# A gate that keeps its logits in PSUM, and the order of work where attention meets the first MoE layer

## The chip, the core and the metric

The kernel runs on one core of one Trainium2 chip. The metric is the device time of one execution in microseconds (us), the median of three. The engines are called by the profile's names: PE multiplies matrices (its weight loads, PEld, overlap it), DVE and POOL do elementwise work, ACT does activations and copies, SP issues DMAs. POOL also issues the indirect DMAs that scatter rows. Each engine has one queue of its own and works through it in order; it waits on semaphores that other engines raise.

## The reference

Three layers follow each other. The first is attention masked by clusters: queries and keys are assigned to the nearest of 16 centroids of their head, and a score counts only where both have the same one.

```python
mask = q_assign[:, :, :, None] == k_assign[:, :, None, :]
scores = np.where(mask, scale * np.matmul(q, k.transpose(0, 1, 3, 2)), -1e9)
attn = np.exp(scores - np.max(scores, axis=-1, keepdims=True))
attn /= np.sum(attn, axis=-1, keepdims=True) + 1e-09
x = np.matmul(attn, v)                 # 2 x 8 heads x 768 tokens x 64
```

The second is a mixture of 8 experts (MoE) over the 1536 tokens with 512 columns. A noisy gate picks two experts for each token:

```python
noisy = x @ w_gate + np.log1p(np.exp(x @ w_noise)) * noise
top2 = np.argpartition(-noisy, 2, axis=1)[:, :2]     # weights: softmax of the two
out[mask] += top2_w[mask, k, None] * (np.maximum(x[mask] @ w1[e], 0) @ w2[e])
```

The third is a soft mixture: 32 slots, each a weighted mean of all tokens, go through 8 experts and are mixed back. The change does not touch it.

## The kernel before, in words

**Attention.** The 16 heads are worked through as 8 pairs `p`, each in 12 steps `t` (two halves `qh` of the queries, six blocks `kc` of the keys). One loop runs over the steps `s0 = 0, 2, ..., 96`, two steps to a turn. A turn emits, in this order: up to three units of masked maxima for a pair to come (`munit`: PE writes `pmx`, L333, and DVE reduces it to `mp`, L338 and L343), the scores of its two steps (`psc`, L372 and L374), the products with V of the two steps before (`av`, L387, into the PSUM tile `pav`), the adds of the exponentials `pt` for the denominators (`add`: `psa` on POOL, `psb` on DVE, L404 and L407), and then what the tables `post` hold for these steps: `ot_evac` (ACT copies `pav` out), `den` (PE sums `psa` and `psb` over partitions into `pden`, L434; DVE takes the reciprocal `rd` from `dt`, L437 to L440), `xout` (PE `px`, L451; DVE writes the tokens' columns `x` and the partial gate logits `gp`, L454 and L457). The last two turns compute no masked maxima.

**Gates.** `gate(q, ...)` returns a list of small operations. Gate 0 covers the six chunks of 128 tokens of the first batch, gates 1 and 2 the three and three of the second. All operations of a gate but four on ACT are DVE operations on SBUF tiles, at line 567. `rank` counts on PE, for each token and expert, the tokens ahead of it (`prank`, L615 to L618). With the ranks, `scatter` (L638) sends rows of `x` to the experts' lists `xg` in DRAM, 128 rows of one chunk and one choice at a time. These operations lie in one list `todo`. `gap(s, n)` takes up to `n` of them out of it, and is called five times in a turn; an integer in the list ends a call, and so spaces the operations.

**First MoE layer.** It has 80 steps in ten jobs of eight; jobs 0 and 1 are the short lists, 256 rows each, of the first experts. A step loads 128 columns' weights (`load_w`), splits them into a high and a low part (`split_hi` on ACT, L833, and `split_lo` on DVE or POOL, L840), multiplies the rows by both (`first`, `ph`, L935), applies the ReLU with high and low parts `H` (L941 and L944), and multiplies back (`second`, `py`, L976). The rows of a job come from `xg` (`load_x`, L856), are transposed on DVE (`prep_t`, L890) and split as well (`prep_h` on ACT, L897; `prep_l`, L903). Before, six steps' weights are split, and the rows of jobs 0 and 1 are loaded and split, in the last pair's turns.

The order of all work is written out by hand in this way; what decides is each engine's own queue.

Of the kernel before, what the change touches and what calls it, by code (L numbers as in the profile page):

```python
# [52 lines left out]
PH, PL = 1, 1  # L53
JT, JN, JH, JL = (0, 2), 2, 2, 3
SP = 1, 3, 5, 7, 8, 9
SL, MX = 1, 96
LT = 6, 8, 9
B1 = 9
B7 = 8
B2 = 1  # L60
TF = (0, 0), (0, 1)
RATE = 2, 1, 1, 1, 2, 3, 1, 2, 1, 1, 4, 1, 3
ORD, U1, Z1, R1, Z0 = (1, 1, 1, 0, 1, 0, 1, 1), 3, 8, 4, 2
M2S = 14, 15, 16, 18, 20
MS = 10, 10, 12, 14, 18
G0, GN, KS = 55, 3, 64

# [17 lines left out]
class Attention:  # L85
# [294 lines left out]
    def av(self, p, t):  # L380
        nc, g = self.nc, self.g
        qh, kc = divmod(t, 6)
        pt = self.ptile[p, t]
        if kc == 0:
            self.avp[p, qh] = g.psum.tile([128, 512], F32, tag="av", name="pav")
        for hh in range(2):
            nc.tensor.matmul(self.avp[p, qh][64 * hh:64 * hh + 64, :384], self.vt[p][:, hh, kc, :],  # L387
                             pt[:, hh, :], start=(kc == 0), stop=(kc == 5))

    def add(self, p, t):  # L390

# [28 lines left out]
    def bank(self, p, qh, name):  # L420
        g = self.g
        if p == NP - 1 and qh == 0:
# [39 lines left out]
class Dispatch:  # L462
# [68 lines left out]
    NFILL = (NSL // 128 + 1) // 2 + (NTOK + NTRASH) // 256  # L531

    def gate(self, q, first, n):

        nc, g, xp = self.nc, self.g, self.g.xp
        b = first // (NCK // B)
# [3 lines left out]
        T = {}  # L540
        place = g.place if q == 0 else g.again

        def t(name, *shape, dt=F32):
            if name not in T and q != 1:
# [3 lines left out]
                names = " ".join("abc"[:len(shape)])  # L548
                a = place(m) if dt is F32 else place(m // 2).bitcast(dt)
                T[name] = a.rearrange(f"p ({names}) -> p {names}", **dict(zip("abc", shape)))  # L550
# [54 lines left out]
        op(TTn, wcol(2), TT, wcol(1), op=OP.mult)  # L605
        out.append(3 if b == 0 else 1)
# [22 lines left out]
        op(TR, Q, W2, axis=AX.X, op=OP.add)  # L629
        if b == 0:  # L630
            op(dv.memset, c1[:, 0:NREG], 0.0)
        op(dv.tensor_copy, self.idx[:, :, cs], Q)
# [143 lines left out]
class MoE1:  # L776
# [567 lines left out]
def body(tc, qk, q2, k2, v2, cent, wgn, noise, w12, phi, v12, out):  # L1344
    nc = tc.nc
    with ExitStack() as ctx:
# [93 lines left out]
        for p in range(-1, NP):  # L1440
# [24 lines left out]
            if p >= 0:  # L1465
                for qh in range(2):
                    at(post, s0 + 6 * qh + 6, A.ot_evac, p, qh)
                    for s, fn in zip(LT if p == NP - 1 else (8, 10, 12), (A.total, A.den, A.xout)):
                        at(post, s0 + 6 * qh + s, fn, p, qh)
# [22 lines left out]
        mix(G0, gates[0][0], [], 1)  # L1492
        for f in gates[0][1]:
            todo += [(G0, None)] * GN + [(G0, f)]
        half = len(todo)

        a, z = gates[1][0], [f for f in gates[2][0] if type(f) is not int]
        i = next(i for i, f in enumerate(a) if type(f) is int and i > 10) - 13
        a, x = a[:i], [f for f in a[i:] if type(f) is not int]
        y, z = z[:21], z[21:]  # L1500
        mix(MX, a, [], 1)
        turns = y[:2] + x[:3] + y[2:6] + x[3:6]
        x, y = x[6:], y[6:]
        while x or y:
            turns += x[:1] + y[:1]
            x, y = x[1:], y[1:]
        mix(99, turns, [], 1)
        k = next(i for i, f in enumerate(z) if f.__name__ == "rank")
        mix(99, z[:k] + [1] + z[k:], gates[1][1], 3)
        mix(99, [], gates[2][1], 1)  # L1510
        half = len(todo) - half
        quota = {1: (8, 16), 2: (14, 14), 3: (14, 14)}

# [22 lines left out]
        def load_x(j):  # L1536
            assert len(todo) <= half, (len(todo), half)
            M1.load_x(j)

        for j in range(2):  # L1540
            at(post, s0 - 4, load_x, j)
            s = s0 + JT[j]
            for i in range(JN):
                at(post, s + i, M1.prep_t, j, i, JN)
                at(post, s + i + JH, M1.prep_h, j, i, JN)
                at(post, s + i + JL, M1.prep_l, j, nc.vector if i % 2 else nc.gpsimd, i, JN)
        end = 12 * NP + 2
        for s0 in range(0, end, 2):
            k = RATE[s0 // 2 - 28] if 56 <= s0 < 82 else 1 if s0 < KS else 3 if s0 < 12 * NP else 0
            units = pre.get(s0, []) + pre.get(s0 + 1, [])  # L1550
# [9 lines left out]
            gap(s0, k)  # L1560
            if s0 == 12 * NP:
                M1.first(0)
            for s in (s0 - 2, s0 - 1):
                if 0 <= s < 12 * NP:
                    A.av(*divmod(s, 12))
                    A.add(*divmod(s, 12))
            for s in (s0, s0 + 1):
                for fn, a in post.get(s, ()):
                    fn(*a)
                gap(s0, k)  # L1570
        late = [x for s in sorted(post) if s >= end for x in post[s]]
        c_at.close()
# [6 lines left out]
        for j in range(2):  # L1579
            at(prep, 5 + j, M1.prep_m, j)  # L1580
        for j in range(2, len(M1.jobs)):
            s, n, eng = PREP[j if j in PREP else 4]
# [7 lines left out]
        for s in range(ns):  # L1590
# [12 lines left out]
            if s < NREG * NF:  # L1603
                gap(1000 if s else 98, quota.get(s, (8, 8))[0])
            if s == ns - 1:
# [3 lines left out]
            elif s < ns - 3 and s != NREG * NF - 1:  # L1609
                M1.second(s)  # L1610
            if s < 2:
                fn, a = late[s]
                fn(*a)
            if s < NREG * NF:
                gap(1000 if s else 98, quota.get(s, (8, 8))[1])
            if s == OV:
# [106 lines left out]
```

## Time and profile before

| what | us |
|---|---|
| median of three executions | 644.04 (643.37 to 644.43) |
| the profiled execution | 650.09 |
| its span, first to last instruction | 648.3 |
| PE busy in the span | 614.9 (95%) |
| DVE, ACT and POOL busy in the span | 409.0, 311.3 and 289.3 |

The rows come from the one profiled execution, and the times from others. The mean granted clock of PE in it was 0.981 of full speed. With PE busy for 95% of the span, its idle time is what an engine beside it can cost.

### The profile page before, as it was taken

The page shows a single profiled execution, that of the slowest core. Times are in us where ns is not written, and L with a number is a line of the kernel's source. Part 1 is how long each engine was busy: PE and PEld are TensorE (multiplying, and loading weights), DVE is VectorE, ACT ScalarE, POOL GpSimd, SP SyncE. Part 2 cuts the span into 40 slices and gives each one's busy share as a digit, 9 for nine tenths or more (in the row PEclk, how much of TensorE's full clock was granted, in tenths as well). Part 3 has the DMA queues.
Part 4 walks back from the last instruction along what each step waited for, and adds up shares of the span by engine and source line. Part 5 has one row for each costly group of instructions (what it writes and reads, how often), then busy time and mean ns, then how long its engine had stood idle before and what let it go on. Part 6 is the DMA issues. An engine that isn't in the chain of part 4 may idle for free. (4 is left out here: it accounts for less than half of the span.)

```text
span 648.3 us, 11039 instructions
## 1 busy us (share of the span) xinstructions
PE 614.9 (95%) x3967; PEld 472.8 (73%) x3967; DVE 409.0 (63%) x871; ACT 311.3 (48%) x444; POOL 289.3 (45%) x256
## 2 busy tenths in 40 slices
PE   7899999999799999789999999999999999998996
PEld 5567666676566657667888888888888888875544
DVE  6667888778965798566554445554544557645632
ACT  5576585765556582245334334443534445533002
POOL 3899676866758793543124033251423403110100
PEclk8699999999899999989999999999999999999999
DMA  8392845727255713478944829879796868978995
GB/s 317 76 267 79 287 149 179 252 89 275 95 191 167 209 66 131 156 223 232 196 133 110 218 98 272 298 255 258 278 281 234 167 207 276 321 269 271 425 398 198
DMA packets 62890, 139.47 MB, mean 215 GB/s; under 512 B 15280, under 2 KB 30832, under 8 KB 60784
## 3 DMA queue, kind: packets, MB, share of 16 engines
q1 hardware_dynamic: 56944, 125.31, 58.3%
q0 software_dynamic: 5888, 13.42, 9.5%
q8 instruction: 32, 0.52, 0.3%
q14 instruction: 26, 0.21, 0.1%
HBM read 108.18 MB, written 28.42 MB: 211 GB/s over the span
## 5 line engine op out<-in xcount | busy, mean ns | idle before, releaser
L976 PE MATMUL py<-ring,H 128*128 128x512 f32 (+1 forms) x686 | 172.9, 396 | 5.3 <-issue 3.5
L840 DVE TENSOR_TENSOR ring<-wr,ring 128x1024 fp32r<-128x1024 f32 (+1 forms) x77 | 93.5, 1214 | 100.4 <-ACT ring L833 99.5
L976 PEld LDWEIGHTS py<-ring,H 128*128 128x128 f32 (+1 forms) x686 | 123.9, 184 | 32.5 <-issue 3.8
L833 ACT ACTIVATE ring<-wr 128x1024 fp32r<-128x1024 f32 x77 | 81.5, 1059 | 91.7 <-PE py L976 83.6
L377 ACT ACTIVATE pt<-psc 128x768 f32<-128x768 f32 x96 | 77.2, 811 | 71.1 <-PE psc L374 60.8
L984 POOL DMA_INDIRECT x2acc<-y,mdi x31 | 50.2, 1621 | 104.4 <-ACT y L1009 97.6
L387 PE MATMUL pav<-pt,vt 128*64 128x384 f32 x384 | 73.6, 505 | 0.0
L941 ACT ACTIVATE H<-ph 128x256 fp32r<-128x256 f32 (+7 forms) x80 | 36.7, 459 | 75.9 <-PE ph L935 60.9
L338 DVE TENSOR_REDUCE mp<-pmx 128x1 f32<-128x512 f32 x96 | 63.2, 676 | 15.3 <-PE pmx L333 14.4
L935 PE MATMUL ph<-XS1a,ring 128*128 128x240 f32 (+3 forms) x288 | 67.8, 325 | 0.0
L407 POOL TENSOR_TENSOR psa<-psa,pt 128x768 f32<-128x768 f32 x32 | 61.9, 1936 | 4.7 <-ACT pt L377 2.5
L935 PE MATMUL ph<-XS0a,ring 128*128 128x432 f32 (+3 forms) x252 | 63.2, 332 | 0.1
L944 DVE SCALAR_TENSOR_TENSOR H<-ph,H 128x384 fp32r<-128x384 f32 (+2 forms) x120 | 43.4, 389 | 26.3 <-ACT H L941 20.6
L935 PEld LDWEIGHTS ph<-XS1a,ring 128*128 128x128 f32 x288 | 47.7, 188 | 3.6 <-DVE ring L840 0.2
L935 PE MATMUL ph<-XS0b,ring 128*128 128x256 f32 (+3 forms) x192 | 48.2, 325 | 0.8 <-DVE ring L840 0.6
L935 PE MATMUL ph<-XS1b,ring 128*128 128x240 f32 (+3 forms) x192 | 46.1, 313 | 0.8 <-DVE ring L840 0.8
L935 PEld LDWEIGHTS ph<-XS0a,ring 128*128 128x128 f32 x252 | 43.2, 188 | 4.0 <-issue 1.2
L903 POOL TENSOR_TENSOR XS0b<-xr,XS0a 128x512 fp32r<-128x512 f32 (+1 forms) x9 | 17.1, 1901 | 64.5 <-ACT XS0a L897 64.5
L387 PEld LDWEIGHTS pav<-pt,vt 128*64 128x64 f32 x384 | 23.5, 137 | 24.8 <-issue 19.3
L333 PE MATMUL pmx<-even 96*128 96x512 f32 (+1 forms) x96 | 34.0, 415 | 6.2 <-DVE mp L338 4.3
L343 DVE TENSOR_REDUCE mp<-pmx 128x2 f32<-128x512 f32 x48 | 33.0, 689 | 5.5 <-PE pmx L333 5.0
L638 POOL DMA_INDIRECT xg<-x,idx x24 | 25.9, 1077 | 21.1 <-DVE xr L567 14.8
(338 smaller groups left out, 1023.7 us busy)
## 6 DMA issues: line engine op xcount, KB each, us to landing
wr<-in_w SPq DMA_DIRECT2D x80, 512.0 KB
v<-in_v SPq DMA_DIRECT2D x9, 2048.0 KB
xg<-xr SPq DMA_DIRECT2D x14, 512.0 KB
wr<-in_qk SPq DMA_DIRECT2D x8, 768.0 KB
early<-in_q SPq DMA_DIRECT2D x8, 768.0 KB
early<-in_k SPq DMA_DIRECT2D x8, 768.0 KB
x2acc<-xr SPq DMA_DIRECT2D x8, 512.0 KB
vt<-in_v SPq DMA_DIRECT2D x8, 384.0 KB
```

What stands on the lines that cost most here:

```text
L333: nc.tensor.matmul(o, self.BQ[i][:96, qh, hh, 128 * c:128 * c + 128], self.BK[i][:96, hh, ks], start=True, stop=True)
L338: nc.vector.tensor_reduce(mp[:, 0, col:col + 1], ps, axis=AX.X, op=OP.max)
L377: nc.scalar.activation(pt, ps[:, :, :384], AF.Exp, scale=SCALE)
L387: nc.tensor.matmul(self.avp[p, qh][64 * hh:64 * hh + 64, :384], self.vt[p][:, hh, kc, :], pt[:, hh, :], start=(kc == 0), stop=(kc == 5))
L407: eng.tensor_tensor(s, s, pt.pop((p, t)), op=OP.add)
L833: self.nc.scalar.activation(self.ring[s][0], self.wr[s], AF.Copy)
L840: nc.vector.tensor_tensor(lo[:, :n], wr[:, :n], f32(hi)[:, :n], op=OP.subtract)
L935: nc.tensor.matmul(ph[:, :u], a[:, 128 * c:128 * c + 128], x[:, c, :u], start=(c == 0 and i == 0), stop=(c == 3 and i == 2))
L941: nc.scalar.activation(HH[:, :u], ph[:, :u], AF.Relu)
L944: nc.vector.scalar_tensor_tensor(o[:, :b - a], ph[:, a:b], 0.0, f32(HH)[:, a:b], op0=OP.max, op1=OP.subtract)
L976: nc.tensor.matmul(o, x, y, start=(f == 0 and i == 0), stop=(f == NF - 1 and i == 2))
L984: st = nc.gpsimd.indirect_dma_start(out=out, out_offset=bass.IndirectOffsetOnAxis(ap=di, axis=0), in_=y, in_offset=None, compute_op=OP.add)
```

## The change

Gate 0 becomes a function of its own. Its logits, and the working tile beside them, lie in PSUM: in the columns 384 to 512 of the bank whose columns 0 to 384 hold `pav`. That bank is now allocated once and used by all pairs. Sixteen operations stay on DVE, some twenty go to POOL, and integers space the list.

Of the twelve scatters of gate 0 two stay where the gate ends, and ten are set into the last pair's turns (`SC`, steps 82 to 90). `load_x` of jobs 0 and 1 follows them at step 91 (it was 80). Job 0 is prepared at steps 94 to 96, all `prep_l` on DVE, and job 1 not before the MoE steps 2 to 4. Four steps' weights are split ahead, where it was six.

In the last half of the last pair the last `pt` is not added on DVE: `pden` takes it as a third term. `den` and `xout` of that half come before the first MoE step, where they were behind it. The first operations of gate 1 come at the steps 94 to 97, the rest up to its `rank`, and four more, around the first MoE step. Five filler matmuls ahead of gate 1's `rank` are gone.

```diff
+        if (p, t) == (0, 0):
+            bank = g.psum.tile([128, 512], F32, tag="av", name="pav")
+            self.avb, g.spare = bank[:, :384], bank[:, 384:]
         if kc == 0:
-            self.avp[p, qh] = g.psum.tile([128, 512], F32, tag="av", name="pav")
+            self.avp[p, qh] = self.avb
...
-        if kc == first:
+        if kc == first or (p, t) == (NP - 1, 11):
             return
...
+        if (p, 6 * qh + 5) in self.ptile:
+            parts.append(self.ptile.pop((p, 6 * qh + 5)))
...
+    def gate0(self, n):
...
+        PL, PW = (lambda i=i: g.spare[:, 8 * n * i:8 * n * i + 8 * n].rearrange("p (c e) -> p c e", e=E) for i in range(2))
...
+        op(TR, U, gl(1), axis=AX.X, op=OP.add)
+        op(TR, PL, gl(0), axis=AX.X, op=OP.add)
+        out.append(1)
+        op(act, U, U, lambda: AF.Exp)
+        out.append(1)
+        op(PS, W, U, 1.0, None, op0=OP.add)
+        out.append(3)
...
+        op(PT, N, N, self.noise[:, :n], op=OP.mult)
+        out.append(3)
+        op(TTn, PL, N, PL, op=OP.add)
+        top(M0, PL)
+        op(TTn, PW, PL, lambda: bcn(M0()), op=OP.is_equal)
+        op(TTn, PW, PW, bce(self.iode), op=OP.mult)
+        top(V0, PW)
+        op(TTn, oh[0], PW, lambda: bcn(V0()), op=OP.is_equal)
+        op(STT, PL, oh[0], -1e30, PL, op0=OP.mult, op1=OP.add)
+        op(PS, wcol(0), V0, -1.0, float(E), op0=OP.mult, op1=OP.add)
...
-            for i in range(5 if q == 1 else 0):
-                nc.tensor.matmul(ps[:, 384:], g.ident, g.ident, start=True, stop=True)
...
-        n = 512 if self.short[self.steps[s][0]] and not 6 <= s < 13 and s < DL else 1024
+        n = 512 if self.short[self.steps[s][0]] and 13 <= s < DL else 1024
...
+        for f, s in zip(gates[0][1][2:], SC):
+            at(post, s0 + s, f)
...
-            at(post, s0 - 4, load_x, j)
...
+            at(post, s0 + JX, load_x, j)
+        for i in range(JN):
+            at(post, s0 + JT[0] + i, M1.prep_t, 0, i, JN)
+            at(post, s0 + JT[0] + i + 1, M1.prep_h, 0, i, JN)
+            at(post, s0 + JT[0] + i + 1, M1.prep_l, 0, nc.vector, i, JN)
...
-            if s0 == 12 * NP:
-                M1.first(0)
...
+            if s0 == 12 * NP:
+                gap(s0, 30)
...
+        gap(1000, lead[0])
+        M1.first(0)
+        gap(1000, lead[1])
```

The first place is DVE's queue in the middle of gate 0. Before, the gate's operations (L567) and the maxima (`mp`) alternate, and the gate's take SBUF tiles (`xr`, `ohe`) alone:

```order
L567 SCALAR_TENSOR_TENSOR xr<-ohe,xr 128x48
L338 TENSOR_REDUCE mp<-pmx 128x1
L567 TENSOR_SCALAR x<-xr 128x6
L338 TENSOR_REDUCE mp<-pmx 128x1
L567 TENSOR_REDUCE xr<-xr 128x6
L343 TENSOR_REDUCE mp<-pmx 128x2
L567 TENSOR_TENSOR xr<-xr 128x48
```

Now the same part reads, with the gate at line 571 and the maxima at 339 and 344:

```order
L339 TENSOR_REDUCE mp<-pmx 128x1
L571 TENSOR_REDUCE xr<-pav 128x6
L339 TENSOR_REDUCE mp<-pmx 128x1
L571 TENSOR_TENSOR pav<-pav,xr 128x48
L344 TENSOR_REDUCE mp<-pmx 128x2
L571 TENSOR_TENSOR pav<-pav,iode 128x48
```

The working tiles are called `pav` now, by the bank they share, and the one-column operation on `x` has gone to POOL.

The second place is PE's queue two turns further on, with the semaphores that each instruction waits for. Before, the products with V (L387) follow the third unit of the maxima (L333) with no wait of their own:

```order
L333 MATMUL pmx<-even 128x256 [waits DVE_49]
L333 MATMUL pmx<-even 128x256
L387 MATMUL pav<-pt,vt 64x384 x4
L451 MATMUL px<-iw,ot 128x160 [waits DVE_49,PE_49]
```

Now they are at line 391, behind the unit at 334:

```order
L334 MATMUL pmx<-even 128x256 [waits DVE_49]
L334 MATMUL pmx<-even 128x256
L391 MATMUL pav<-pt,vt 64x384 [waits DVE_49]
L391 MATMUL pav<-pt,vt 64x384 x3
```

The products wait for DVE here, for the last gate operation emitted ahead of them; this stands in four turns. The third place is PE's queue at the change from attention to MoE. Before:

```order
L387 MATMUL pav<-pt,vt 64x384 x4
L935 MATMUL ph<-XS0a,ring 128x256 x12
L387 MATMUL pav<-pt,vt 64x384 x4
L935 MATMUL ph<-XS0a,ring 128x256 x12
L976 MATMUL py<-ring,H 128x512 x6
L434 MATMUL pden<-psa,sel 32x96 x8
L434 MATMUL pden<-psb,sel 32x96 x8
L935 MATMUL ph<-XS0a,ring 128x256 x12
L976 MATMUL py<-ring,H 128x512 x6
L451 MATMUL px<-iw,ot 128x160 x3
L935 MATMUL ph<-XS0a,more 128x256 x12
L613 MATMUL prank<-ident 128x128 x5
```

And now, with `pden` at line 440, `px` at 457, `ph` at 1043, `py` at 1084 and the rank's matmuls at 725 to 728:

```order
L391 MATMUL pav<-pt,vt 64x384 x8
L440 MATMUL pden<-psa,sel 32x96 x8
L440 MATMUL pden<-psb,sel 32x96 x8
L440 MATMUL pden<-pt,sel 32x96 x8
L457 MATMUL px<-iw,ot 128x160 x3
L1043 MATMUL ph<-XS0a,ring 128x256 x24
```

All of attention stands ahead of the first `ph` now, and `ph` of two steps stands ahead of the rank. On DVE the last rows ahead of that `ph` are these, with the `dt` to `gp` of the last half between five operations of gate 1 and the low part `XS0a`:

```order
L679 TENSOR_TENSOR ohe<-w,v 128x24
L679 SCALAR_TENSOR_TENSOR l<-ohe,l 128x24
L443 STREAM_TRANSPOSE dt<-pden 128x96
L445 TENSOR_SCALAR rd<-dt 128x6
L446 RECIPROCAL rd<-rd 128x6
L460 TENSOR_TENSOR x<-px,rd 128x3x2x32 x2
L463 TENSOR_TENSOR gp<-px,rd 128x3x32
L1011 TENSOR_TENSOR XS0a<-xr,XS0a 128x4x4x32
```

The `XS0a` row is the second half of job 0's low part, which the first `ph` reads; before, it stood on POOL and DVE several turns earlier.

## Rows read from the trace of the kernel before

**Rows 1.** Page, part 5: one instruction group, with count, busy time, mean
```profile
L840 DVE TENSOR_TENSOR ring<-wr,ring 128x1024 fp32r<-128x1024 f32 (+1 forms) x77 | 93.5, 1214 | 100.4 <-ACT ring L833 99.5
```

**Rows 2.** Stretches of six loop turns; the columns are in the first line
```profile
core 0: us, PE busy (x) PEld busy (x) DVE busy (x) ACT busy (x) POOL busy (x), PEclk, DMA share, GB/s
113.82:140.89 27.07, 26.89 (x191) 18.16 (x190) 21.07 (x42) 17.68 (x25) 18.83 (x11) 1.00 0.54 181
140.89:172.52 31.63, 27.57 (x206) 18.42 (x205) 26.62 (x54) 20.27 (x30) 22.31 (x13) 1.00 0.48 164
172.52:201.16 28.64, 28.19 (x206) 19.26 (x205) 21.21 (x58) 15.77 (x23) 19.51 (x14) 0.94 0.53 182
201.16:228.59 27.43, 25.55 (x193) 17.58 (x192) 17.65 (x32) 15.79 (x21) 22.99 (x16) 1.00 0.68 198
```

**Rows 3.** Timeline of PE: start, duration, instruction, idle before it and releaser
```profile
172.09 0.51 PE L333 MATMUL pmx<-even 96*128 96x256 f32 x2 [3.33 <-DVE mp L338]
```

**Rows 4.** Timeline of DVE under the first gate, same columns
```profile
153.43 1.45 DVE L567 TENSOR_REDUCE xr<-gp 128x96 f32<-128x768 f32 x1
...
169.80 1.63 DVE L567 SCALAR_TENSOR_TENSOR xr<-ohe,xr 128x48 f32<-128x48 f32 x1
171.36 0.68 DVE L338 TENSOR_REDUCE mp<-pmx 128x1 f32<-128x512 f32 x1
171.96 1.33 DVE L567 TENSOR_SCALAR x<-xr 128x6 f32<-128x6 f32 x1
```

**Rows 5.** Stretch of 5 us around that idle time, columns as above
```profile
170.00:175.00 5.00, 2.91 (x11) 0.99 (x12) 5.00 (x7) 1.17 (x2) 4.92 (x3) 0.79 0.15 40
```

**Rows 6.** Timeline of PE, an undisturbed turn
```profile
118.08 1.51 PE L387 MATMUL pav<-pt,vt 128*64 128x384 f32 x8
```

**Rows 7.** Timeline of DVE, the same turn
```profile
118.19 0.69 DVE L343 TENSOR_REDUCE mp<-pmx 128x2 f32<-128x512 f32 x1
```

**Rows 8.** Waits of PE, 140 to 250 us: for whom, total, times, longest
```profile
PE psc L372 <- DMA oddb<-nmt: 0.6, 1, 0.6
```

**Rows 9.** Timeline of PE, last turns of attention and first MoE steps
```profile
238.34 0.45 PE L372 MATMUL psc<-oddb 97*128 97x384 f32 x1
...
242.48 0.54 PE L434 MATMUL pden<-psb,sel 128*32 128x96 f32 x16 [0.56 <-DVE psb L407]
...
245.38 1.51 PE L387 MATMUL pav<-pt,vt 128*64 128x384 f32 x8
246.82 1.69 PE L935 MATMUL ph<-XS0a,ring 128*128 128x256 f32 x12
...
258.83 1.28 PE L613 MATMUL prank<-ident 128*128 128x128 f32 x10
261.89 0.17 PE L615 MATMUL prank<-mb,tri 128*128 128x24 bf16 x1 [1.78 <-DVE mb L567]
```

**Rows 10.** Timeline of DVE, last turns of attention and the second gate
```profile
244.06 1.79 DVE L903 TENSOR_TENSOR XS0b<-xr,XS0b 128x512 fp32r<-128x512 f32 x1
245.77 0.27 DVE L437 STREAM_TRANSPOSE dt<-pden 128x96 f32<-128x96 f32 x1
...
248.01 0.61 DVE L454 TENSOR_TENSOR x<-px,rd 128x192 f32<-128x192 f32 x2
...
250.65 0.94 DVE L404 TENSOR_TENSOR psb<-pt 128x768 f32<-128x768 f32 x1
...
252.84 0.80 DVE L567 TENSOR_REDUCE lg<-gp 128x48 f32<-128x384 f32 x1
...
256.37 0.18 DVE L567 TENSOR_TENSOR l<-l,u 128x24 f32<-128x24 f32 x1
256.59 0.18 DVE L567 TENSOR_TENSOR l<-l,noise 128x24 f32<-128x24 f32 x1
```

**Rows 11.** Timeline of PE, two single idle times
```profile
211.17 0.50 PE L333 MATMUL pmx<-oddb 96*128 96x256 f32 x2 [1.88 <-DVE mp L338]
...
277.40 1.89 PE L976 MATMUL py<-ring,H 128*128 128x512 f32 x6 [3.46 <-issue]
```

More of the change, by code (lines that the diff above doesn't have):

```diff
@@ L53 @@
 PH, PL = 1, 1
[L54 to L57, printed above, removed]
+JX, JT, JN = 7, (10, 2), 2
+SC = -2, 0, 0, 0, 2, 2, 4, 4, 6, 6
+LEAD = 5, 16
+SP = 1, 3, 5, 7
+SL, MX = 1, 94
+LT = (6, 8, 9), (6, 6, 6)
 B1 = 9
@@ L61 @@
 TF = (0, 0), (0, 1)
-RATE = 2, 1, 1, 1, 2, 3, 1, 2, 1, 1, 4, 1, 3
 ORD, U1, Z1, R1, Z0 = (1, 1, 1, 0, 1, 0, 1, 1), 3, 8, 4, 2
@@ L65 @@
 MS = 10, 10, 12, 14, 18
-G0, GN, KS = 55, 3, 64
+G0 = 55
 class Ctx:
@@ L421, in bank @@
         g = self.g
-        if p == NP - 1 and qh == 0:
+        if p == NP - 1 and (qh == 0 or name == "pden"):
             return g.psum.tile([128, 512], F32, tag="mx", name=name, bufs=2)
@@ L533, in gate @@
     def gate(self, q, first, n):
+        if q == 0:
+            return self.gate0(n)
         nc, g, xp = self.nc, self.g, self.g.xp
@@ L540, in gate @@
         T = {}
-        place = g.place if q == 0 else g.again
         def t(name, *shape, dt=F32):
@@ L548, in t @@
                 names = " ".join("abc"[:len(shape)])
-                a = place(m) if dt is F32 else place(m // 2).bitcast(dt)
+                a = g.again(m) if dt is F32 else g.again(m // 2).bitcast(dt)
                 T[name] = a.rearrange(f"p ({names}) -> p {names}", **dict(zip("abc", shape)))
@@ L605, in gate @@
         op(TTn, wcol(2), TT, wcol(1), op=OP.mult)
-        out.append(3 if b == 0 else 1)
+        out.append(1)
         def rank():
@@ L629, in gate @@
         op(TR, Q, W2, axis=AX.X, op=OP.add)
-        if b == 0:
-            op(dv.memset, c1[:, 0:NREG], 0.0)
         op(dv.tensor_copy, self.idx[:, :, cs], Q)
@@ L1467, in body @@
                     at(post, s0 + 6 * qh + 6, A.ot_evac, p, qh)
-                    for s, fn in zip(LT if p == NP - 1 else (8, 10, 12), (A.total, A.den, A.xout)):
+                    for s, fn in zip(LT[qh] if p == NP - 1 else (8, 10, 12), (A.total, A.den, A.xout)):
                         at(post, s0 + 6 * qh + s, fn, p, qh)
@@ L1492, in body @@
         mix(G0, gates[0][0], [], 1)
-        for f in gates[0][1]:
-            todo += [(G0, None)] * GN + [(G0, f)]
+        todo += [(G0, f) for f in gates[0][1][:2]]
         half = len(todo)
[L1497 to L1504, printed above, removed]
+        a, z = [f for f in gates[1][0] if type(f) is not int], [f for f in gates[2][0] if type(f) is not int]
+        at_rank = lambda x: next(i for i, f in enumerate(x) if f.__name__ == "rank")
+        n1, n2 = at_rank(a), at_rank(z)
+        mix(MX, a[:LEAD[0]], [], 1)
+        mix(96, a[LEAD[0]:LEAD[1]], [], 1)
+        x, y = a[n1 + 1:], z[9:n2]
+        turns = a[LEAD[1]:n1] + z[:9] + a[n1:n1 + 1]
+        while x:
             turns += x[:1] + y[:1]
@@ L1507, in body @@
         mix(99, turns, [], 1)
-        k = next(i for i, f in enumerate(z) if f.__name__ == "rank")
-        mix(99, z[:k] + [1] + z[k:], gates[1][1], 3)
+        mix(99, y, gates[1][1], 2)
+        mix(99, z[n2:], [], 1)
         mix(99, [], gates[2][1], 1)
         half = len(todo) - half
-        quota = {1: (8, 16), 2: (14, 14), 3: (14, 14)}
+        quota = {0: (19, 9), 1: (9, 0), 2: (14, 14), 3: (14, 14)}
+        lead = n1 - LEAD[1] + 1, 4
         def gap(s, n):
@@ L1538, in load_x @@
             M1.load_x(j)
+        for f, s in zip(gates[0][1][2:], SC):
+            at(post, s0 + s, f)
         for j in range(2):
-            at(post, s0 - 4, load_x, j)
[L1542 to L1546, printed above, removed]
+            at(post, s0 + JX, load_x, j)
[3 more added lines that the diff above has]
+            at(post, s0 + JT[0] + i + 1, M1.prep_l, 0, nc.vector, i, JN)
         end = 12 * NP + 2
         for s0 in range(0, end, 2):
-            k = RATE[s0 // 2 - 28] if 56 <= s0 < 82 else 1 if s0 < KS else 3 if s0 < 12 * NP else 0
+            k = 1 if s0 < MX else 0
             units = pre.get(s0, []) + pre.get(s0 + 1, [])
@@ L1569, in body @@
                     fn(*a)
-                gap(s0, k)
-        late = [x for s in sorted(post) if s >= end for x in post[s]]
+                gap(s0, 30 if s == MX + 1 else k)
+        assert max(post) < end
+        gap(1000, lead[0])
+        M1.first(0)
+        gap(1000, lead[1])
         c_at.close()
@@ L1580, in body @@
             at(prep, 5 + j, M1.prep_m, j)
+        for i in range(JN):
+            at(prep, JT[1] + i, M1.prep_t, 1, i, JN)
+            at(prep, JT[1] + i + 1, M1.prep_h, 1, i, JN)
+            at(prep, JT[1] + i + 1, M1.prep_l, 1, nc.vector, i, JN)
         for j in range(2, len(M1.jobs)):
@@ L1603, in body @@
             if s < NREG * NF:
-                gap(1000 if s else 98, quota.get(s, (8, 8))[0])
+                gap(1000, quota.get(s, (8, 8))[0])
             if s == ns - 1:
@@ L1610, in body @@
                 M1.second(s)
-            if s < 2:
-                fn, a = late[s]
-                fn(*a)
             if s < NREG * NF:
-                gap(1000 if s else 98, quota.get(s, (8, 8))[1])
+                gap(1000, quota.get(s, (8, 8))[1])
             if s == OV:
```

75 lines of the change are left out of this document (added).

## The prediction

> **What bounds the kernel now.** I read the page first, then stretches of the attention loop, then the waits and the timelines of PE and DVE at the two places that the change touches. Six turns of the loop take 27.07 us where no gate runs, with PE busy for 26.89 of them; they take 31.63 and 28.64 us in the two stretches that hold gate 0, and 27.43 in the next [rows 2]. PE is the bound there, so whatever makes it wait is time. Gate 0 adds 31.63 + 28.64 - 2 x 27.07 = 6.13 us. Most of it is one wait: PE sits idle for 3.33 us until DVE has a maximum `mp` ready [rows 3]. DVE is late because small operations hold it up. An operation on 128x48 elements took 1.63 us, and one on 128x6 took 1.33, against 0.18 for one on 128x24 in the later gates, while POOL was busy for 4.92 of 5 us; the maxima, which read PSUM, kept their 0.68 in between [rows 4, 5, 10]. In the same stretch the mean granted clock is 0.79 [rows 5], a part of it at the lower of the two levels, behind the idle time.
>
> At the end of attention PE loses less: 0.58 us for a transposed maximum [rows 8], then 0.56 for `psb`, 1.28 for the fillers, and 1.78 before gate 1's rank [rows 9].
>
> **Gate 0.** The change takes operations of this kind off DVE or gives them one PSUM input and at most one in SBUF, like the maxima that were not held. I therefore take the whole 6.13 us as removed. What comes back is a new wait. `pav` and the gate's tiles share a bank, and in four turns PE's products with V now wait for a DVE operation. Today they don't: in an undisturbed turn `pav` starts at 118.08 and the maximum of the same unit at 118.19, for 0.69 us [rows 6, 7]. In three of the four turns the gate's operation stands behind that maximum, so PE waits for 0.11 + 0.69 and 0.2 for the operation itself: 1.0 us each. In the fourth it is a reduction of half the 1.45 us one [rows 4], ahead of the third maximum: about 0.7. That makes 3.7 us. I take 3.2, because a PE held here finds the next maxima ready, which it now and then waits for. The ends are 2.0 (half of the waits taken from waits that PE has anyway) and 5.0 (DVE late by another 0.3 in each). Behind the waiting `pav` stand the scores of the next turn, and behind them ACT's exponentials, so nothing else fills the hole.
>
> One page of the Trainium skill speaks against the change here. "PSUM — Partial Sum Buffer", section "PSUM bank collisions raise a hardware error", says that two engines may not use one bank in the same partitions at once, disjoint columns included, that the chip does not arbitrate, and that software has to order them. The order of the changed program agrees; no run here shows the collision itself. If columns 384 to 512 were free of columns 0 to 384, the 3.2 us would drop out of the sum; by the page they stay.
>
> Some twenty small operations go to POOL, at about 0.2 us each 4 us (DVE's time for the like [rows 10]). POOL is busy for 22.31 and 19.51 us in these stretches [rows 2], and the integers in the list leave it more than half a turn; I cost them at nothing. If that cover fails, DVE's first addition to the logits waits for POOL, and the maxima queued behind it wait too: up to one POOL add.
>
> **The last pair.** Scatters, loads and the preparation of job 1 leave the turns before step 88, so the 0.58 us wait goes [rows 8]. From then on DVE sets the time. I count from the first score of the last full turn but one (238.34, X = 0).
>
> PE's own work up to the first `ph`: before, it starts at 246.82, 8.48 us on, with 0.56 of idle time in it: 7.92. The second group of `pav` now comes first: 246.82 - 245.38 = 1.44 [rows 9]. The three-term `pden` and `px` come first too: 1.1 and 0.6, estimates from `pav`'s time and their narrower columns. That is 11.1 us.
>
> DVE's chain: PE reaches the `psb` half of `pden` at 242.48 - 0.56, X = 3.6, so `dt` starts at 3.8. Then `dt` to `rd` 0.6 (0.27 for the first and two small ones), the low part of step 3's weights 1.2 [rows 1], `x` and `gp` 0.7 [rows 10], the first transposition 0.65, ACT's copy 0.6, the first low part 0.65, the second transposition 0.65 (all 512 columns, estimated at half of the 1214 ns for 1024 in rows 1). X is now 8.9. The reduction to `lg` takes 0.80 and `psb` 0.94 [rows 10], with one small operation and ACT between them 0.45: 11.05. Eleven gate operations that depend on each other follow every 0.215 us (256.37 to 256.59 [rows 10]): 13.4. Last come `dt` to `rd` 0.6, `x` and `gp` 0.8, the second low part 0.65, and the semaphore: 15.8. PE waits for 15.8 - 11.1 = 4.7 us. It is in two pieces, about 1.7 where `pden` needs `psb`, and 3 before `ph`.
>
> The ends of this 4.7: 3.6, if the pieces overlap better than I chain them, and 7.0, if the low parts of weights and rows are held as one was before, 1.79 instead of 0.65 [rows 10], while POOL adds `psa`. After an idle time of 3.33 us the clock was down [rows 3, 5], after one of 1.78 I see nothing; 3 lies near the first, and costs 0 to 1.0 (a fifth of 5 us). I take 0, because the rank behind it then has slack.
>
> The other terms here: 8 more matmuls for `pden` 0.4. Gate 1's rank comes two `ph` later, when DVE is done with `mb`, and waits for nothing; gate 2's rank 0.3 (0 to 1.5: some 24 interleaved operations at half the 0.215). Removed: 0.56 + 1.78 + 1.28 = 3.62. Net: 4.7 + 0.4 + 0.3 - 3.62 = +1.8.
>
> At nothing: steps 4 and 5, no longer split ahead, and the whole low parts on DVE, because DVE has most of a step's 2.9 us free; without that cover 1.2 us a step [rows 1]. The row loads go out on SP behind three weight loads and the last scatters, and I see the rows land at about the time of the first transposition; each us later is a us of the chain.
>
> **Sum.** -6.1 + 3.2 - 0.6 + 1.8 = -1.7 us. The profiled execution took 650.09 us for a span of 648.3, and would take 648.4. It is 6.05 above the median. Two idle times in it, 1.88 and 3.46 us [rows 11], look to me like part of that difference: the semaphores came late while scatters and weight loads ran, and the second waits for nothing the profile names. I leave them out, and carry the -1.7 to the median: 642.3 us.
>
> **Rivals.**
> - *The wait moves to the end of attention, and costs more.* Slower. One mechanism: DVE's chain before the first `ph` is held by POOL's adds. Four operations with two SBUF inputs are in it; at 1.1 us more each the idle time is 9.1 and the time 646.7. For it: DVE was held so in exactly these turns [rows 10]. Against it: the last POOL adds may be done by then. It turns the sign when the idle time passes 6.4 us, and is slower by over 0.2% from 7.7.
> - *The bank wait eats the gain.* If the four waits cost 5.0, the time is 644.1, no change. For it: the chain maximum, operation, `pav` has no cover at all; against it: PE waits for DVE in these turns anyway.
> - *The late semaphores are in every execution, and go with the scatters.* With scatters spread, one or both of 1.88 and 3.46 us vanish: 637 to 640.5. For it: both idle times stand beside scatters. Against it: the profiled execution alone is 6 us long, and gate 1's scatters are still dense.
>
> **How the numbers follow.** A difference under 0.2%, 1.3 us, can't be told from none. My forecast has 0.47 (within 640.5 to 643.7; 0.37 of it faster, 0.10 the same), the moved wait 0.18 (slower), the bank wait 0.22 (0.02 faster, 0.18 the same, 0.02 slower), the late semaphores 0.13 (faster). That gives faster 0.52, the same 0.28, slower 0.20. Below 638.5 lies about 0.08, most of the third rival's depth, and above 645.8 about 0.11, the worse part of the first: these are the ends of the range.
>
> **What would show it.** Right: no idle time of PE over 1.5 us in the gate's stretch, its two sets of six turns at about 57.4 us together instead of 60.27, no small gate operation over 0.5 us on DVE, four idle times near 1 us in front of `pav` with DVE as releaser, and 3 to 6 us of idle time of PE between 238 and the first `ph`, part of it put down to `psb`, part to the low part of the rows. Wrong: `pav` not waiting for DVE (then 3 us faster), transpositions that wait for the row loads, a rank that waits by more than 1.5 us, or new idle time beside the scatters in the last pair.

## The result and the profile after

The change makes the kernel slower. The median is 651.45 us (650.46 to 653.11, four executions) against 644.23 for the kernel before, and the ratio is 1.0105 (95% interval 1.0072 to 1.0138). The forecast was 642.3 with a range of 638.5 to 645.8: wrong in sign and in size. The profiled execution of the change took 651.29 us, its span 649.5.

The stretches of six turns, cut at the same groups of `pav` as [rows 2], which they answer to:

```profile
core 0: us, PE busy (x) PEld busy (x) DVE busy (x) ACT busy (x) POOL busy (x), PEclk, DMA share, GB/s
113.34:140.43 27.09, 26.92 (x191) 18.19 (x190) 21.08 (x42) 17.68 (x25) 18.84 (x11) 1.00 0.54 181
140.43:168.95 28.52, 27.00 (x206) 18.55 (x205) 20.21 (x43) 18.15 (x28) 19.30 (x17) 1.00 0.53 182
168.95:199.37 30.42, 26.77 (x205) 18.73 (x204) 18.94 (x53) 17.62 (x26) 20.20 (x18) 1.00 0.39 128
199.37:224.79 25.42, 25.42 (x193) 17.60 (x193) 17.60 (x37) 15.93 (x21) 19.06 (x19) 1.00 0.40 141
```

The two stretches of gate 0 take 28.52 + 30.42 = 58.94 us, where they took 31.63 + 28.64 = 60.27: the gate's part gains 1.3 us. The last stretch has lost the 1.88 us of idle time [rows 11] that stood beside the old scatters. The waits of PE show where the rest went (for whom, total, times, longest):

```profile
PE pden L440 <- DVE psb L408: 9.1, 1, 9.1
PE pav L391 <- DVE pav L571: 2.4, 2, 1.5
...
PE ph L1043 <- DVE XS0a L1011: 1.3, 1, 1.3
PE pav L391 <- DVE ohe L571: 1.1, 1, 1.1
PE pav L391 <- ACT pt L378: 1.0, 1, 1.0
PE pav L391 <- DVE xr L571: 0.9, 1, 0.9
PE prank L621 <- POOL odda L306: 0.7, 1, 0.7
```

The waits of `pav` for DVE are the forecast's bank waits: 2.4 + 1.1 + 0.9 = 4.4 us in four turns. They stand where PE waited for the maxima in [rows 3]. The first line is new, and it is the largest part of the result: one wait of 9.06 us, for `psb`. `psb` itself is a short addition. What held it is on DVE's timeline:

```profile
240.17 0.25 DVE L463 TENSOR_TENSOR gp<-px,rd 128x96 f32<-128x96 f32 x1
249.17 0.71 DVE L998 STREAM_TRANSPOSE xr<-xr 128x512 f32<-128x512 f32 x1 [8.76 <-DMA xr<-xg]
...
252.94 0.95 DVE L408 TENSOR_TENSOR psb<-pt 128x768 f32<-128x768 f32 x1
```

The first transposition of job 0's rows (L998) waits 8.76 us for the DMA that loads them. `psb` (L408) is ready to run but stands behind it in DVE's queue, and `pden` and everything after stand behind `psb`. The rows come behind their scatters. On POOL the first scatter goes out after 4.80 us of idle time, which the profile puts down to a weight load, and the twelfth starts at 238.81:

```profile
210.75 1.23 POOL L746 DMA_INDIRECT xg<-x,idx  x1 [4.80 <-DMA wr<-in_w]
...
238.81 1.76 POOL L746 DMA_INDIRECT xg<-x,idx  x1 [0.30 <-issue]
```

SP issues the row loads when that scatter has landed, at 243.67, nearly 5 us after its start:

```profile
227.60 10.41 SPq L937 DMA_DIRECT2D wr<-in_w  x3
243.67 1.81 SPq L964 DMA_DIRECT2D xr<-xg  x4
```

SP's three weight loads ahead of them are out at 238.01, so it is the scatter that the row loads wait for here. The rows are there at 249.17, 5.5 us after their loads went out. PE, from the end of its denominators' first half:

```profile
253.95 0.87 PE L440 MATMUL pden<-psb,sel 128*32 128x96 f32 x16 [9.06 <-DVE psb L408]
...
256.95 0.61 PE L1043 MATMUL ph<-XS0a,ring 128*128 128x256 f32 x1
258.83 4.80 PE L1043 MATMUL ph<-XS0a,ring 128*128 128x256 f32 x23 [1.26 <-DVE XS0a L1011]
263.47 0.19 PE L725 MATMUL prank<-mb,tri 128*128 128x24 bf16 x1
```

The granted clock falls with the idle time and stays low behind it. In four of the 3 us stretches (columns as in the first fence):

```profile
244.00:247.00 3.00, 0.71 (x18) 0.32 (x16) 0.00 (x0) 0.00 (x0) 0.29 (x1) 0.80 0.76 173
...
250.00:253.00 3.00, 0.00 (x0) 0.00 (x0) 2.13 (x5) 0.77 (x2) 0.00 (x0) 0.50 0.76 208
...
259.00:262.00 3.00, 3.00 (x15) 3.00 (x16) 1.93 (x10) 0.62 (x3) 0.00 (x0) 0.50 0.00 0
262.00:265.00 3.00, 3.00 (x20) 2.73 (x20) 1.36 (x6) 0.91 (x4) 0.00 (x0) 0.85 0.01 3
```

It is 0.50 from 247 to 262, the lower of the two levels. The 24 matmuls of the first two `ph` then take from 256.95 to 263.47 with 1.26 of waiting in it, 5.3 us. Before, the first two groups of twelve (the first starts at 246.82 [rows 9]) took 1.61 and 1.53, to the instruction behind each:

```profile
248.43 1.51 PE L387 MATMUL pav<-pt,vt 128*64 128x384 f32 x8
249.87 1.69 PE L935 MATMUL ph<-XS0a,ring 128*128 128x256 f32 x12
251.40 1.55 PE L976 MATMUL py<-ring,H 128*128 128x512 f32 x6
```

### The profile page after: what moved, and what is told of

It reads as the page before. It is cut to its first block, busy times and chain, and to the rows that moved or that the text cites. A ratio compares the mean times of both kernels' runs of the same rounds, so it can differ in the third digit from the quotient of the medians.

```text
span 649.5 us, 11042 instructions
## 1 busy us (share of the span) xinstructions
PE 612.1 (94%) x3973; PEld 473.3 (73%) x3973; DVE 397.8 (61%) x856; ACT 311.6 (48%) x444; POOL 281.5 (43%) x268
## 5 line engine op out<-in xcount | busy, mean ns | idle before, releaser
L1043 PE MATMUL ph<-XS0a,ring 128*128 128x432 f32 (+3 forms) x252 | 65.1, 343 | 1.4 <-DVE XS0a L1011 1.3
L1043 PEld LDWEIGHTS ph<-XS0a,ring 128*128 128x128 f32 x252 | 45.2, 200 | 4.3 <-DVE XS0a L1011 1.6
L1043 PE MATMUL ph<-XS0b,ring 128*128 128x256 f32 (+3 forms) x192 | 46.6, 316 | 0.8 <-DVE ring L948 0.6
L746 POOL DMA_INDIRECT xg<-x,idx x24 | 29.4, 1226 | 33.8 <-DVE inv L679 22.7
```

What stands on the lines that cost most here:

```text
L1043: nc.tensor.matmul(ph[:, :u], a[:, 128 * c:128 * c + 128], x[:, c, :u], start=(c == 0 and i == 0), stop=(c == 3 and i == 2))
```

## The experiments

Times are medians, and ratios are to the kernel before, timed beside each batch of runs. It took 646.1 us beside the first four runs below, 651.1 beside the next three, 645.1 beside the four in the table and 653.6 beside the old gate. The first two batches have the same chip number, so it isn't shown that the chip is what differs; here a batch is called an occasion. Runs of different occasions are therefore compared through their profiles first.

**Scatters as early as the gate allows.**

```diff
-        todo += [(G0, f) for f in gates[0][1][:2]]
+        todo += [(G0, f) for f in gates[0][1]]
...
-        for f, s in zip(gates[0][1][2:], SC):
-            at(post, s0 + s, f)
```

> The change with one thing undone: all twelve scatters of gate 0 leave as soon as the gate has their indices, instead of ten of them in the last pair's turns; the row loads stay at step 91. Theory A (the rows of job 0 come late because their last scatter is late, 238.81 us, and DVE's queue stands behind the first transposition): the row loads issue when SP is free of its third weight load, at about 238 instead of 243.7, so PE's idle time before the three-term denominators falls from 9.1 to 3.5 us, and the time by 5.5 us to about 646. Theory B (SP's queue, not the scatters, holds the row loads): the same 5.5 at most if scatters matter, none if the weight loads alone do; then the time stays at 651.5. Theory C (DVE's own chain of work is what PE waits for): no gain, PE waits as long, on psb with DVE busy.

Measured: 660.67 us, ratio 1.0218 (1.0192 to 1.0245). Counted from the first score of the last full turn but one (233.94 in the change, 245.20 here), the row loads go out after 5.3 us instead of 9.7, the first transposition starts after 11.3 instead of 15.2, and the wait for `psb` falls to 6.5 us. The last scatter now starts 19.5 us ahead of the loads (at 230.98), and the loads go out as soon as SP's third weight load is out:

```profile
238.13 12.30 SPq L937 DMA_DIRECT2D wr<-in_w  x3
250.53 1.87 SPq L964 DMA_DIRECT2D xr<-xg  x4
```

So the scatters hold the loads for some 4.4 us in the change, and behind that SP's weight loads hold them, which is theory B's part. Another wait, of 7.4 us, appears in front of the scores:

```profile
PE psc L373 <- ACT pt L378: 8.7, 2, 7.4
PE pden L440 <- DVE psb L408: 6.5, 1, 6.5
```

ACT can't write the next `pt`, since POOL has not added the last ones to `psa`:

```profile
226.99 1.51 ACT L378 ACTIVATE pt<-psc 128x768 f32<-128x768 f32 x2 [10.44 <-POOL psa L408]
```

and POOL has not, because the add stands behind five scatters in its queue, 1.29 us apart, of which this is the last:

```profile
224.12 0.98 POOL L746 DMA_INDIRECT xg<-x,idx  x1 [0.30 <-issue]
225.17 1.79 POOL L408 TENSOR_TENSOR psa<-pt 128x768 f32<-128x768 f32 x1
```

So POOL's queue is a second place where a scatter holds attention. In the change, where the scatters are spread, this wait is not there, and the rows are later. None of the three theories had this wait.

**Rows loaded early too.**

```diff
-JX, JT, JN = 7, (10, 2), 2
+JX, JT, JN = 2, (10, 2), 2
```

> The scatters early as in the run before, and the row loads of jobs 0 and 1 at step 86 instead of 91, ahead of two of the weight loads on SP. Theory A: DVE no longer waits for rows at the first transposition (8.8 us before), PE's idle time at the end of attention falls from 10.3 us to the 4 to 5 that the prediction's chain of DVE gives, and the time by 5 to 9 us, to 643 to 646. Theory C: no gain beyond 1 us. Rival D (the scatters collide with other work where they stand now): the wait goes, but as much is lost between 205 and 235 us.

Measured: 655.38 us, ratio 1.0153 (1.0117 to 1.0188).

```profile
PE psc L373 <- ACT pt L378: 8.8, 1, 8.8
...
PE pden L440 <- DVE psb L408: 2.4, 1, 2.4
PE ph L1043 <- DVE XS0a L1011: 1.9, 1, 1.9
```

Theory A's wait is gone: `pden` and `ph` wait for 2.4 + 1.9 = 4.3 us, where the forecast's chain of DVE gave 4.7. Rival D holds as well: as much is lost to POOL's queue before. The time is therefore no test of theory A; the two waits are.

**Job 0's preparation behind the tail of attention.** Scatters and loads as in the change.

```diff
-            at(post, s0 + JT[0] + i, M1.prep_t, 0, i, JN)
-            at(post, s0 + JT[0] + i + 1, M1.prep_h, 0, i, JN)
-            at(post, s0 + JT[0] + i + 1, M1.prep_l, 0, nc.vector, i, JN)
+            at(post, s0 + 12, M1.prep_t, 0, i, JN)
+            at(post, s0 + 13, M1.prep_h, 0, i, JN)
+            at(post, s0 + 13, M1.prep_l, 0, nc.vector, i, JN)
```

> Scatters and row loads as in the change; only the transpositions and splits of job 0's rows go behind psb, gate 1's eleven operations, dt, x and gp on DVE (steps 96 and 97). Theory A says the rows arrive at 249.2 us whatever stands in front of them, so attention's tail is then worked off under the wait: the wait at the denominators goes (9.1 to under 2 us), the first ph waits for the rows instead and starts at about 252.5 instead of 258.8: 6 us faster, about 645.5. Theory C: the chain is only reordered, and the gain is under 1 us.

Measured: 645.62 us, ratio 0.9991 (0.9974 to 1.0007). Theory A's number was 645.5; that it fits to a tenth is chance (the same kernel took 646.73 on another occasion, below). The wait for `psb` is 0.4, and the first `ph` starts at 251.92 instead of 256.95:

```profile
PE ph L1043 <- ACT XS0a L1005: 4.5, 1, 4.5
...
PE pden L440 <- DVE psb L408: 0.4, 1, 0.4
```

```profile
251.92 0.58 PE L1043 MATMUL ph<-XS0a,ring 128*128 128x256 f32 x1 [4.54 <-ACT XS0a L1005]
```

The rows arrive no sooner, but DVE uses the time. `psb` now runs at 244.50 instead of 252.94, and the transpositions wait for their rows 0.62 us:

```profile
244.50 0.94 DVE L408 TENSOR_TENSOR psb<-pt 128x768 f32<-128x768 f32 x1
...
249.90 1.30 DVE L998 STREAM_TRANSPOSE xr<-xr 128x512 f32<-128x512 f32 x2 [0.62 <-DMA xr<-xg]
```

**Gate 0's tiles in SBUF**, on top of the run with early rows.

```diff
-        PL, PW = (lambda i=i: g.spare[:, 8 * n * i:8 * n * i + 8 * n].rearrange("p (c e) -> p c e", e=E) for i in range(2))
+        PL, PW = (lambda k=k: t(k, n, E) for k in ("pl", "pw"))
```

> The run with early rows, with gate 0's two working tiles in SBUF instead of the free columns of the bank of the products with V. Bank theory (the four waits of those products for DVE, 4.4 us in the change's trace, come from the shared bank alone): the four waits go, and the time falls by 3 to 4 us against the run with early rows. Contention theory (DVE operations with SBUF operands alone are held while POOL adds, which is what the PSUM tiles avoid): small gate operations of over 0.5 us come back on DVE, the maxima are late, and the time rises by 1 to 3 us against that run.

Measured: 652.86 us, ratio 1.0121 (1.0087 to 1.0156), 2.5 us less than that run. The four bank waits are gone, and PE waits for the maxima instead:

```profile
PE pmx L334 <- DVE mp L339: 2.4, 2, 1.9
```

Both theories hold in part: 4.4 us go, 2.4 come, and operations of the gate on 128x48 elements take up to 1.71 us on DVE again. The clock accounts for much of the rest: from 179 to 193 us its mean is 0.88 of full speed here, and 1.00 with the tiles in the bank. PE reaches the turn at 207 us 0.4 us sooner; the larger part of the 2.5 arises later, in front of the scores, and isn't the gate's.

**Gate 0 at twice the pace**, scatters and row loads early again.

```diff
+        for f in gates[0][1]:
+            todo += [(G0, None)] * 3 + [(G0, f)]
...
-            k = 1 if s0 < MX else 0
+            k = 2 if 56 <= s0 < 84 else 1 if s0 < MX else 0
...
-JX, JT, JN = 7, (10, 2), 2
+JX, JT, JN = 0, (10, 2), 2
```

> The change, but gate 0 takes two operations a call from the list in the steps 56 to 83 instead of one, all twelve scatters follow it with three empty places between them as in the kernel before, and the rows are loaded at step 84, ahead of the weight loads. Theory A (the gate is stretched by 20 us, and with it everything that needs its indices: scatters, row loads, the first transposition, and by DVE's queue the end of attention): indices are ready near 185 to 190 us, the rows are there before 235, PE's wait of 9.1 us before the denominators falls to about 2 and the one before the first ph stays at 1 to 2: 5 to 7 us faster than the change, 644.5 to 646.5. Theory C: no gain over 1 us. Rival E (the gate needs its wide spacing): PE loses 2 us or more between 152 and 190 us against the change.

Measured: 649.42 us where before took 651.1, ratio 0.9986 (0.9959 to 1.0012).

```profile
PE pmx L334 <- ACT oddb L299: 3.7, 2, 2.3
PE pden L440 <- DVE psb L408: 2.5, 1, 2.5
PE pmx L334 <- DVE mp L339: 2.3, 3, 1.5
```

At the end of attention PE waits 2.5 + 1.3 us, near theory A's 2 and 1 to 2. But the time is not the 644.5 to 646.5 that theory A gave: waits of PE for the maxima and for ACT come, 6.0 us together, among the gate and its scatters. Twelve turns from the start of the gate take 62.57 us in the profiled execution, against 58.94 in the change, as rival E has it in kind; the run changes the pace of the gate and the place of its scatters together. On the same occasion it is 4.8 us slower than the run told below with rows a turn earlier.

**Gate 1's operations behind the low part**, on top of that: `LEAD = 5, 5` instead of `5, 16`.

> The run before with eleven operations of gate 1 behind the low part of the rows on DVE instead of ahead of the last half's dt, x and gp. If DVE's chain sets the start of the first ph once the rows are early, as the prediction had it, the chain is 2.4 us shorter, of which the rank then gives back 1 to 1.5: 1 us faster than the run before. If the rows or PE set it, nothing or slower by what the rank waits.

Measured: 652.01 us, ratio 1.0018 (0.9985 to 1.0051): no gain that can be seen. `pden` still waits 2.5 and `ph` 1.3, and gate 2's rank 0.5. So moving the eleven operations out of DVE's chain shortened neither wait; the forecast counted 2.4 us for them. DVE stands idle for as long in their place, 1.19 + 1.18 us, for PE's `pden` and `px`:

```profile
255.98 0.28 DVE L443 STREAM_TRANSPOSE dt<-pden 128x96 f32<-128x96 f32 x1 [1.19 <-PE pden L440]
...
257.87 0.62 DVE L460 TENSOR_TENSOR x<-px,rd 128x192 f32<-128x192 f32 x2 [1.18 <-PE px L457]
```

PE's own way from `psb` over `pden` and `px` to `x` is as long as the eleven operations. It runs at the lower clock here: the granted clock is 0.50 from 256 to 262 us, and `px` takes 1.97 us, where it took 1.08 a turn before.

**Rows a turn earlier**, on top of the preparation behind the tail.

```diff
-SC = -2, 0, 0, 0, 2, 2, 4, 4, 6, 6
+SC = -2, 0, 0, 0, 2, 2, 4, 4
-JX, JT, JN = 7, (10, 2), 2
+JX, JT, JN = 5, (10, 2), 2
...
-        todo += [(G0, f) for f in gates[0][1][:2]]
+        todo += [(G0, f) for f in gates[0][1][:4]]
...
-            at(post, s0 - 10, M1.load_w, i)
+            at(post, s0 - 5, M1.load_w, i)
...
```

> The run with job 0's preparation behind the tail (645.6), with four scatters in the list, the other eight a turn earlier, the first four weight loads at step 79 instead of 74 (in the change the first scatter stood 4.8 us until such a load had landed), and the rows loaded at step 89. If the rows still set the start there, first scatter at 206 instead of 211, rows 3 to 4 us earlier, and the time 0.5 to 1 us better, since DVE's chain is then 0.6 us behind them. If weights come late for their split instead, DVE waits for ACT's high parts and the time rises by 2 us or more.

Measured: 644.58 us where before took 651.1, ratio 0.9926 (0.9908 to 0.9945). The first scatter starts at 207.21 (206 was expected), SP issues the row loads at 238.38 instead of 243.67, and the transpositions no longer wait for their rows:

```profile
207.21 1.58 POOL L746 DMA_INDIRECT xg<-x,idx  x1 [2.94 <-issue]
```

```profile
248.23 1.29 DVE L998 STREAM_TRANSPOSE xr<-xr 128x512 f32<-128x512 f32 x2
```

The first scatter still comes after 2.94 us of idle time, though the next weight loads go out behind it, at 212.70, and the profile names nothing that it waits for. Moving the weight loads gave back 1.9 of the 4.80 us; what the rest is stays open.

**Four kernels on one chip.** The change, the preparation behind the tail, the rows a turn earlier, and the last with gate 0's tiles in SBUF.

> The change itself once more, on one chip with the next three. The kernel before took 644 to 646 us where the change and the first runs were timed, and 651 where the last were, with two idle times of PE beside its scatters in both of its profiles. If these idle times are what differs and the change has none, the change stays at 651 to 652 wherever it runs: slower by 1% where the kernel before takes 644 to 646, no different where it takes 651. If the chip as a whole is slower there, the change is slower by the same 1% on every chip.

> The run with job 0's preparation behind the tail, on the same chip as the change. Theory A: 6 us faster than the change here too (651.5 to 645.6). If most of that came from the chip, the two are within 2 us.

> The run with rows a turn earlier, on the same chip as the run it was made from. Its profile is 2.4 us shorter than that one's, 1 us of it before the first gate: 1 to 2 us faster than it, 644 to 645, if the rows a turn earlier are worth what the two profiles say; equal to it within 0.5 if not.

> The run with rows a turn earlier, with gate 0's two working tiles in SBUF. The first such pair (runs with early rows) showed the four bank waits gone, 4.4 us, a 2.6 us wait for the maxima in their place, and 0.4 us gained up to 208 us. If that holds: 0 to 1 us faster than the run with rows a turn earlier. If the 2.5 us by which the first pair differed in their times come from the bank: 2 to 3 us faster.

Measured, with before at 645.12 us:

| kernel | us | ratio to before, 95% interval |
|---|---|---|
| the change | 651.68 | 1.0086 (1.0052 to 1.0120) |
| preparation behind the tail | 646.73 | 1.0006 (0.9984 to 1.0027) |
| rows a turn earlier | 645.31 | 1.0003 (0.9983 to 1.0022) |
| the same, tiles in SBUF | 644.63 | 0.9990 (0.9968 to 1.0012) |

The change is 5.0 us slower than the kernel that differs from it only in where job 0's preparation stands in the queues of DVE and ACT, and 6.4 slower than the one with rows a turn earlier. The last three can't be told from before here. The first expectation stays undecided: before took 645.1 here, and there both of its readings give 1%. At the end of attention PE still waits 5.6 us with rows a turn earlier, within the forecast's 3.6 to 7.0, and now for the rows' high part:

```profile
PE ph L1043 <- ACT XS0a L1005: 3.8, 1, 3.8
...
PE pden L440 <- DVE psb L408: 1.8, 1, 1.8
```

Rows a turn earlier brought 1.4 us, inside what was expected but inside the spread too. The tiles in SBUF brought 0.7, which the intervals don't separate. So keeping the logits in PSUM shows no gain: what the new gate is worth (next run) must lie in its other parts, the operations on POOL and the spacing, which no run takes apart.

**The old gate in the new order.** Rows a turn earlier, with gate 0 as it was, one operation a call.

```diff
-        if q == 0:
-            return self.gate0(n)
...
```

> The run with rows a turn earlier, with gate 0 as it was before: all on DVE and in SBUF, one operation a call; everything else as in that run. This gives the new gate's own worth. The prediction gave it 2.9 us (6.1 of the old gate's cost, less 3.2 of new waits): then this run takes 647 to 649, and PE comes to 200 us some 3 us later. The traces so far say 1.3 us, or less: then 645 to 647. If the old gate's cost was the faster pace at which it was called, not the SBUF tiles, there is no difference at all.

Measured: 647.51 us (647.03 to 652.5), ratio 0.9891 (0.9855 to 0.9927), where before took 653.6. The same order with the new gate took 644.58 and 645.31 on two other occasions, so the new gate is worth 2.2 to 2.9 us here, if the occasion doesn't matter to them; its upper end is the prediction's 2.9. The pace at which the gate is called is the same in both, so it isn't the pace. PE waits for the maxima again, 5.6 us up to 215 us in place of the 4.4 of the bank and 0.7 for POOL, in the profiled execution, which took 652.5; twelve turns from the start of the gate take 62.72 us there:

```profile
PE pmx L334 <- DVE mp L339: 5.6, 4, 1.7
```

**The kernel before, two more profiles.**

> The kernel before once more, for a second profile. If the two idle times of PE at 211 and 277 us (1.88 and 3.46) belong to every execution, both are there again and the profiled execution takes some 650 us. If they belong to that one execution, as the prediction took it, they are gone, the span is 642 to 644 us, and the profile of the change has to be compared with a span some 6 us shorter.

> The kernel before a third time, for a profile beside its times on the chip that is drawn. If the two idle times of PE beside its scatters belong to some chips only, they are gone in a profile whose chip gives it 644 to 646 us and there in one whose chip gives it 650; if they are in every execution, they are there at 645 too, and then they don't explain the 6 us between the chips.

Measured: 650.02 and 653.46 us, on occasions where before's median was 651.1 and 653.6. The idle time near 211 us is there both times, 1.85 and 1.87 us. The one in the MoE steps is 2.76 us in the second profile and 7.05 in the third:

```profile
276.83 1.66 PE L976 MATMUL py<-ring,H 128*128 128x512 f32 x6 [2.76 <-issue]
```

```profile
281.87 2.93 PE L976 MATMUL py<-ring,H 128*128 128x512 f32 x6 [7.05 <-ACT H L941]
```

Both profiles come from occasions that gave before some 650 us or more, and the first profile took 650.09 itself. No profile of before from an execution of 644 to 646 us exists, so that the idle times are what separates the occasions remains argued: 4.3 us more in one of them goes with 3.4 us more in the time. The profiles of the change, of the preparation behind the tail and of the rows a turn earlier have no idle time of that kind.

## Why the prediction was wrong

**The step that failed** stood under "At nothing": "The row loads go out on SP behind three weight loads and the last scatters, and I see the rows land at about the time of the first transposition; each us later is a us of the chain." The rule in its second half was right, and the first half was 8.8 us off. DVE was ready for the transposition at 240.4 us, 6.5 after the first score of that turn (forecast 6.3), and the rows came 15.2 after it. The forecast gave no duration to the landing of a scatter or of the loads: it is 238.81 to 243.67 for the last scatter and 5.5 us more for the loads. The first scatter was 4.8 us late besides; how much of that reaches the last one no run shows. The low part of the rows then let `ph` go on 24.9 us after that score, where the forecast's chain had 15.8: 9.1 us later. That this is nearly the 9.2 us by which the time missed the forecast is partly chance, since other terms were off too. The late landing was costed at nothing, and no term or end of the range held it; it stood only among the forecast's own signs of being wrong. With the preparation moved behind the tail and nothing else changed, 5.0 us come back on one occasion, and about 6 between two.

**The idle time at the end of attention**, 4.7 us by the chain on DVE: 4.3 us with early rows (2.4 and 1.9, where the forecast had 1.7 and 3), so the sum held where rows didn't interfere, and its two pieces less well. In the change it was 9.1 + 1.3, with 1.0 more in front of `pav`. But DVE's chain is not the only one: moving eleven gate operations out of it, 2.4 us of its sum, changed neither wait, because PE's `pden` and `px` at the lower clock take as long beside them.

**The clock**, 0 taken and 1.0 as the end: idle for 9 us, it stayed low to 262 us, and cost 5.3 - 3.1 = 2.2 us on the first two `ph`. That is not the late rows' doing alone. With early rows, behind waits of 2.4 and 1.9 us, the clock is at 0.50 from 262 to 265 us, and the same 24 matmuls take 5.1 us: the term was too small by itself, by about 2 us.

**Gate 0**, -6.1 + 3.2 = -2.9: the bank waits were 4.4 us, more than the 3.7 worked out before the discount to 3.2, so the discount did not come. A wait of 0.7 for POOL came beside them. In the trace the part gains 1.3, and the old gate put back costs 2.2 to 2.9 by the times. The rule of the Trainium skill that two engines' accesses to one bank have to be ordered (in "PSUM — Partial Sum Buffer", section "PSUM bank collisions raise a hardware error") agrees with the trace as far as the order goes: the waits are there with the tiles in the bank, 4.4 us, and gone with the tiles in SBUF. No run let the two collide. With the tiles in SBUF operations on DVE take up to 1.71 us again, yet the time does not rise: what PSUM spares on DVE, the shared bank takes back on PE.

**The small terms.** The 0.58 us wait for a transposed maximum is gone: that group of `pav` comes 3.85 us after the one before, where it was 4.45. Gate 1's and gate 2's ranks wait for nothing.

**The rivals.** Slower came true, and by a wait at the end of attention; but not by the rival's mechanism. The low parts of the rows took 0.69 and 0.68 us in the change, not held at all, and that its 9.1 us of idle time equal the measured wait is chance. With rows a turn earlier one operation of the chain is held: the low part of step 3's weights takes 2.24 us instead of 1.20. The bank wait was 4.4, near its 5.0. The third rival's idle times are there in all three profiles of before. Where before takes 651.1 and 653.6, two orders with later scatters are faster than it by 0.7% and 1.1%; where it takes 645.1, the first of them is not.

## What to carry to other kernels

An engine's queue turns one late input into a wait for all that stands behind it: when a load is moved later, find its first reader, and what is queued behind that reader on its engine. Follow a moved transfer to the end, from the queue that issues it over its landing to the load that waits for it, with a measured duration for each, before costing it at nothing. Scatters on the engine that also frees a buffer can hold that buffer: early they cost 7.4 us in front of the scores here, late 9.1 us in front of the denominators.

## What was not expected of the hardware

The kernel before took 644 to 646 us on some occasions and 651 to 654 on others, and the changed order did not follow it: rows a turn earlier took 644.58 us where before took 651.1, and 645.31 where before took 645.1. In two of the three profiles of before ACT waited, while scatters and weight loads ran, for a semaphore whose matmuls on PE had ended earlier, by 3.0 us in the first profile and by 6.6 in the third:

```profile
281.43 0.38 ACT L941 ACTIVATE H<-ph 128x256 fp32r<-128x256 f32 x1 [9.44 <-remote]
```

What delays them was not tried.
